# Lightning attention with a PReLU feed-forward: the written-out order of the first three chunks, written anew

## The chip, the cores and the metric

The kernel runs on one core of a Trainium2 chip. The core has five engines, each with a queue of its own that it works through in order: TensorE (PE, the matmuls; its weight loads are shown as PEld), VectorE (DVE), ScalarE (ACT), GpSimd (POOL) and SyncE (SP, which here only issues DMAs). The metric is the device time of one execution in microseconds (us). Results lie in SBUF, matmuls write into PSUM, and inputs and the output lie in HBM.

## What is computed

The inputs are q, k and v of shape (batch 4, heads 8, positions 768, width 64), one decay factor `lam` per head, and the feed-forward's `w_in` (512 x 2048), `w_out` (2048 x 512) and `alpha` (2048). Attention is linear with a decay, in blocks of 64 positions that hand a state on:

```python
intra = einsum('bhic,bhjc->bhij', qb, kb) * Dmask      # lam ** (i - j) for i >= j, else 0
intra = einsum('bhij,bhjd->bhid', intra, vb)
inter = einsum('bhid,bhde->bhie', qb * lam_pow, kv_state)
out[:, :, sl] = intra + inter
kv_state = lam_block * kv_state + einsum('bhsd,bhse->bhde', kb * rev_pow, vb)
```

The outputs of all heads side by side are the 3072 rows of x (512 wide), and the kernel's output is `g @ w_out` with `h = x @ w_in` and `g = max(h, 0) + alpha * min(h, 0)`, in float32.

## The kernel before

**Tiling.** The positions are taken in blocks of 128 here, two at a time. A chunk `c` (six of them) is 256 positions of two batches, thus 512 rows of x; a *unit* is one chunk, one batch and one half of the heads (four heads), so each chunk has four units, numbered 4c to 4c + 3. Of unit `n`, `units[n]` is the chunk, the batch within it and the half of heads. Units 0 and 1 are the first batch of chunk 0, units 2 and 3 the second; units 4 to 7 are chunk 1, 8 to 11 chunk 2.

**What a unit needs, and which function issues it:**
- `load` (L80): q, k or v of one batch in float32 into `kraw`, `qraw`, `vraw`; all eight heads, or four of them (`half` 0 or 1), by SP's queue or, with "G", by POOL's. `load_v16` (L272): v of one unit, turned into float16 on the way, always by POOL. `load_win`, `load_wout`: a quarter of `w_in` or `w_out`, by POOL.
- `cast` (L261): float32 to float16 of q or k (tile `qk`), on ACT ("A"), DVE ("V") or POOL ("G"), by way of `copy_on` (L246; ACT's instruction is L248, DVE's L250, POOL's L252).
- `transposed` (L328): four transposes of one of q and k on PE (L337) into a PSUM bank and a copy back to SBUF (tile `qkT`). `transposes` (L302) does both at once, on PE or, with "D", by a transposing DMA from SP.
- `key_decayed` (L285): k times its decay (tile `kdec`, L289), on POOL or DVE. `decayed` (L346): q times its decay (tile `qdT`, L351), on POOL, on DVE, or with "P" on DVE straight from the transposes' PSUM bank.
- `score_products` (L380): 16 small matmuls into the PSUM tile `s`, of which there is one (L387); `masked` (L395): `s` times the decay mask, on DVE (L398, tile `sm`). `scores` is both.
- the state of a unit: 8 small matmuls for each of its two blocks (`state_products`, L432); in the first position pair, `states` (L451) then copies the first block's state on ACT (L471) and updates the second block's on DVE (L461, two instructions). `state` does both blocks, into a bank each; `state1` (L516) does one block into one bank. Both first zero the other half of the bank with two matmuls (`beside`, L498).
- the output of a unit: two matmuls with the state (`inter`, L371) and 16 with the masked scores (`intra`, L412), into the PSUM tile `acc`, of which there is one, and a copy of it to `xT` (`attended`, L441) on ACT or DVE.
- `cluster(old, new, eng)` (L474): the output of unit `old` (copied by `eng`), and scores and state of unit `new`, interleaved.

**The feed-forward.** `up(c, f)` (L527) makes 128 of the 2048 hidden columns of a chunk: four matmuls 512 wide (L532), ACT's negative part (L540) and DVE's combination with the slopes (L549). With `bi` it does one batch, half as wide. `down(c, t, part, 4)` (L556) adds a quarter of the hidden columns to one 128-row piece of the output (L562); the last quarter is followed by ACT's copy (L575) and a store by SP. `oma`, one minus the slopes, comes from `slopes` (L235: one small transpose on PE, one DVE instruction L238).

**Constants at the start.** From `lam`, ACT makes the decay vectors with exponentials: `query_decay` (L230), `key_decay`, `state_decay`, `decay_mask`; DVE makes the masks' logarithms (`mask_logs`, L198, two instructions L200 per call, four calls).

**Unread products.** `tick(n, bank)` (L146) and `fill(n, bank)` (L134) are matmuls whose result nobody reads: 128 columns wide (L150) and 512 wide (L138). They occupy PE and nothing else. 16 narrow ones on zeros stand ahead of everything.

**What sets the order.** The kernel is written under a manual schedule: each engine gets its instructions in the order in which the Python calls are made, and only semaphores wait between engines. Lines 633 to 934 are such a list, written out by hand: it interleaves the attention of chunks 0 to 4 (up to unit 18's casts) with the feed-forward of chunks 0 to 2, and says which engine takes each cast, copy or load and which PSUM bank each product goes to. The banks are `h` (two buffers), `op` and `tk` (one each); `s` and `acc` take the rest. From line 936 on a loop does chunks 3 to 5. `gate(i, "out")` (L115) is a tiny load on SP that waits for a part of `w_out`, so that what follows it on SP's queue stays behind.

Of the kernel before, what the change touches and what calls it, by code (L numbers as in the profile page):

```python
# [11 lines left out]
def kernel(  # L12
# [211 lines left out]
    def state_decay():  # L224
        nc.scalar.activation(rdecay, llp, AF.Exp, scale=float(L))
# [298 lines left out]
    G = {}  # L524
# [186 lines left out]
    load_v16(4)  # L711
    up(0, 5, None, "h")
    up(0, 4, 1, "tk")
    up(0, 2, None, "op")
    load(1, 1, "k", 1, "G")
    cast(4, "q16", "V")
    up(0, 3, None, "h")
    up(0, 0, None, "h")
    up(0, 6, None, "op")
# [12 lines left out]
    cast(7, "q16", "G")  # L732
    gate(2, "out")
    load_v16(7)
    transposed(4, 1, "V", "tk")
    cast(5, "q16", "G")
    load(2, 0, "k", 0)
    cast(5, "k16", "A")
    up(0, 11, None, "h")
# [237 lines left out]
```

## Time and profile before

| | |
|---|---|
| three runs | 211.89, 212.13, 212.15 us; median 212.13 |
| profiled execution | 211.88 us, of which 210.1 are the span from the first to the last instruction |
| PE busy | 204.2 us (97%) |
| DVE busy | 134.7 us (64%) |
| ACT busy | 111.5 us (53%) |
| POOL busy | 81.3 us (39%) |
| HBM | 27.27 MB read, 6.29 MB written |

In the profile, L12 is line 12 of the kernel; a helper's line stands for all its calls. A group of instructions has its engine, its operation, its tiles (written tile first), its shape and its count. `[0.35 <-ACT qk L248]` behind a row of the timeline says that the engine stood idle for 0.35 us ahead of it until ACT's instruction at L248 released it. PE's ends are modelled, so successive matmuls overlap in the rows; the distance from start to start is what one takes. The granted clock is PE's clock as a share of its full speed.

### The profile page before, as it was taken

The page shows a single profiled execution, that of the slowest core. Times are in us where ns is not written, and L with a number is a line of the kernel's source. Part 1 is how long each engine was busy: PE and PEld are TensorE (multiplying, and loading weights), DVE is VectorE, ACT ScalarE, POOL GpSimd, SP SyncE. Part 2 cuts the span into 40 slices and gives each one's busy share as a digit, 9 for nine tenths or more (in the row PEclk, how much of TensorE's full clock was granted, in tenths as well). Part 3 has the DMA queues.
Part 4 walks back from the last instruction along what each step waited for, and adds up shares of the span by engine and source line. Part 5 has one row for each costly group of instructions (what it writes and reads, how often), then busy time and mean ns, then how long its engine had stood idle before and what let it go on. Part 6 is the DMA issues. An engine that isn't in the chain of part 4 may idle for free.

```text
span 210.1 us, 5186 instructions
## 1 busy us (share of the span) xinstructions
PE 204.2 (97%) x2131; PEld 109.0 (52%) x2131; DVE 134.7 (64%) x230; ACT 111.5 (53%) x203; POOL 81.3 (39%) x111
## 2 busy tenths in 40 slices
PE   7989999999999999999999999999999999999993
PEld 7666445556444565555555455454554444444453
DVE  7998987456898959899964664664745444444000
ACT  7966697047677046677654554554444443443121
POOL 8999599233743422752880664421000000000000
PEclk9999999999999999999999999999999999999999
DMA  6999999999999979999496794224101101110212
GB/s 166 274 198 252 269 229 200 242 239 263 287 148 290 135 189 194 276 195 260 94 236 156 208 235 104 62 41 100 53 0 53 50 0 50 50 55 0 100 50 100
DMA packets 56315, 32.06 MB, mean 153 GB/s; under 512 B 23508, under 2 KB 52580, under 8 KB 56292
## 3 DMA queue, kind: packets, MB, share of 16 engines
q1 hardware_dynamic: 44788, 22.82, 44.8%
q0 software_dynamic: 11488, 8.91, 24.7%
q8 instruction: 16, 0.26, 0.5%
q14 instruction: 7, 0.06, 0.1%
q10 hardware_dynamic: 16, 0.00, 0.0%
HBM read 27.27 MB, written 6.29 MB: 160 GB/s over the span
## 4 chain that ended last, share of the span: by engine, by line
PE 93%; DVE 3%; ACT 1%; issue 0%; ACTq 0%
PE h_ps L532 40%; PE o_ps L562 34%; PE o_ps L585 7%; PE s L387 4%; PE acc L412 3%; PE acc L371 2%; PE tpx L337 1%; DVE dmask L200 1%; PE acc L432 1%; PE unread L138 1%; ACT L178 1%; DVE sm L398 1%; DVE kdec L289 1%; ACT xT L248 1%; DVE qk L250 0%
## 5 line engine op out<-in xcount | busy, mean ns | idle before, releaser
L549 DVE SCALAR_TENSOR_TENSOR g<-m,oma,h_ps 128x512 f16<-128x512 f32 (+1 forms) x97 | 70.9, 741 | 47.1 <-ACT m L540 44.6
L532 PE MATMUL h_ps<-xT,w_in_sb 128*128 128x512 f16 (+1 forms) x388 | 92.3, 377 | 0.0
L540 ACT ACTIVATE m<-h_ps 128x512 f32<-128x512 f32 (+1 forms) x97 | 57.4, 593 | 51.3 <-PE h_ps L532 51.0
L562 PE MATMUL o_ps<-w_out_sb,g 128*128 128x512 f16 x320 | 79.5, 379 | 0.0
L532 PEld LDWEIGHTS <-w_in_sb 128*128 128x128 f16 x388 | 37.3, 98 | 42.9
L562 PEld LDWEIGHTS <-g 128*128 128x128 f16 x320 | 30.0, 98 | 33.8
L398 DVE TENSOR_TENSOR sm<-s,dmask 128x1024 f16<-128x1024 f32 x24 | 29.3, 1220 | 9.5 <-PE s L387 9.3
L351 POOL TENSOR_TENSOR qdT<-qkT,qdecay 128x512 f16<-128x512 f16 (+1 forms) x19 | 18.9, 999 | 24.1 <-PE h_ps L532 14.6
L289 POOL TENSOR_TENSOR kdec<-kraw,kdecay 128x512 f16<-128x512 f32 x18 | 19.1, 1061 | 13.5 <-DMA kraw<-in_k_dram 13.5
L575 ACT ACTIVATE o_sb<-o_ps 128x512 f32<-128x512 f32 (+2 forms) x26 | 14.7, 565 | 18.1 <-PE o_ps L585 10.9
L248 ACT ACTIVATE xT<-acc 128x512 f16<-128x512 f32 x21 | 12.5, 596 | 18.0 <-PE acc L432 15.5
L461 DVE SCALAR_TENSOR_TENSOR R<-R,rdecay,acc 128x128 f16<-128x128 f16 x56 | 16.1, 339 | 0.5 <-ACT R L471 0.5
L252 POOL CAST v<-vraw 128x512 f16<-128x512 f32 x11 | 6.9, 628 | 21.3 <-DMA vraw<-in_v_dram 21.3
L585 PE MATMUL o_ps<-w_out_sb,g 128*128 128x512 f16 (+2 forms) x96 | 14.1, 308 | 0.0
L585 PEld LDWEIGHTS <-g 128*128 128x128 f16 x96 | 8.1, 98 | 6.1
L387 PE MATMUL s<-qkT 64*64 64x128 f16 x384 | 10.1, 222 | 0.2 <-DVE qkT L250 0.2
L412 PE MATMUL acc<-sm,v 64*64 64x128 f16 x384 | 9.8, 217 | 0.4 <-issue 0.4
L276 POOL DMA_DIRECT2D v<-in_v_dram x12 | 9.3, 780 | 0.2 <-issue 0.2
L371 PEld LDWEIGHTS <-R 128*128 128x128 f16 x80 | 6.2, 98 | 5.5 <-ACT xT L248 0.6
L371 PE MATMUL acc<-qdT,R 128*128 128x128 f16 x80 | 8.4, 220 | 0.4 <-ACT xT L248 0.4
L252 POOL CAST qk<-kraw 128x512 f16<-128x512 f32 x13 | 8.0, 612 | 1.7 <-DVE g L549 1.2
L387 PEld LDWEIGHTS <-qkT 64*64 64x64 f16 x384 | 6.3, 106 | 2.9 <-ACT qk L248 0.4
(69 smaller groups left out, 126.6 us busy)
## 6 DMA issues: line engine op xcount, KB each, us to landing
out_dram<-o_sb SPq DMA_DIRECT2D x23, 256.0 KB, 2.1
kraw<-in_k_dram SPq DMA_DIRECT2D x12, 256.0 KB, 5.0
qraw<-in_q_dram SPq DMA_DIRECT2D x10, 256.0 KB, 5.0
qraw<-in_q_dram SPq DMA_DIRECT2D x4, 512.0 KB, 5.5
w_in_sb<-in_moe_w_in_dram POOLq DMA_DIRECT2D x4, 512.0 KB, 8.5
w_out_sb<-in_moe_w_out_dram POOLq DMA_DIRECT2D x4, 512.0 KB, 10.3
vraw<-in_v_dram SPq DMA_DIRECT2D x4, 512.0 KB, 6.2
kraw<-in_k_dram SPq DMA_DIRECT2D x3, 512.0 KB, 5.1
```

Of the source, the lines that this page charges most:

```text
L289: engine(eng).tensor_tensor(out=kdec, in0=kr, in1=kdecay[:, ds(4 * hh, 4), :].rearrange("p h e -> p e h").unsqueeze(3).to_broadcast([128, ...
L351: engine(eng).tensor_tensor(out=qdT[:, :, :, p], in0=(t["qps"] if eng == "P" else t["qkT"][:, 0])[:, :, :, p], in1=qdecay[:, hh, :, :, p], ...
L371: nc.tensor.matmul(ot[a][:, hp, :].rearrange("p (e j) -> p e j", e=2), lhsT=R[bb, ho, 2 * pbo + a][:, hp].rearrange("p l d -> p (l d)"), r ...
L387: nc.tensor.matmul(t["s"][ds(a * 64, 64), hl, hp, 1 - e, :].rearrange("p (e j) -> p e j", e=2), lhsT=t["qkT"][p, 1, e, hp, ds(a * 64, 64)] ...
L398: nc.vector.tensor_tensor(out=t["sm"].rearrange("p a h x j -> p (a h) x j"), in0=t["s"].rearrange("p a h x j -> p (a h) x j"), in1=mask_of ...
L412: nc.tensor.matmul(ot[a][ds(hl * 64, 64), hp, :], lhsT=t["v16"][p, 2 * hp + hl, e, :], rhs=t["sm"][p, hl, hp, 1 - e, :], start=(2 * pb + a ...
L461: nc.vector.scalar_tensor_tensor(out=R[b, hh, m + 1][:, hp], in0=R[b, hh, m][:, hp], scalar=rdecay[:, 2 * hh + hp : 2 * hh + hp + 1], in1= ...
L532: nc.tensor.matmul(h_ps[:, 0:n] if bi is None else h_ps[:, 0:n].rearrange("p (e j) -> p e j", e=2), lhsT=w_in_sb[:, gi, ts(f, 128)], rhs=x ...
L540: nc.scalar.activation(m[:, 0:n], h_ps[:, 0:n], AF.Relu, scale=-1.0)
L549: nc.vector.scalar_tensor_tensor(out=g, in0=mv, scalar=oma[:, f : f + 1], in1=hv, op0=ALU.mult, op1=ALU.add)
L562: nc.tensor.matmul(o_ps, lhsT=lhs(c, f, t), rhs=w_out_sb[:, f, :], start=(f == 0), stop=(f == NF - 1),)
L585: nc.tensor.matmul(o_ps[:, 0:n], lhsT=lhs(c, f, t), rhs=w_out_sb[:, f, ds(x, n)], start=(f == 0), stop=(f == NF - 1),)
```

## The change

Lines 633 to 934, the list, are replaced by a list of the same calls in another order and partly on other engines, banks and queues; no function is changed. The calls that make up the work of chunks 0 to 2 are the same but for these points:

- the narrow unread products, 24 and 22 in two places, are 6 and 56 ahead of the first transpose; the wide ones, seven, are three
- unit 3's state is two `state1` calls in place of one `state`; unit 6's scores and state are calls of their own in place of a part of a cluster
- the first output (unit 1) is copied by ACT in place of DVE, unit 0 keeps ACT
- q of chunk 0's second batch is loaded in two halves in place of whole; of chunk 1 and later, some loads are whole that were halves and the other way round, and one key half of unit 6 goes by SP's queue in place of POOL's
- v of unit 11 is loaded as float32 and cast on POOL in place of being turned on the way
- casts, decayed keys, decayed queries and copies change engines in many places; `slopes` stands ahead of the first scores; `up` of one tile of chunk 1 is done in two halves

The diff from its start to the first `up`, and the later places that the prediction speaks of:

```diff
--- before
+++ after
                 a[i]()
                 i += 1
 
+    load(0, 1, "k", 0, "G")
+    query_decay(3, 1)
     query_decay(2, 1)
-    load(0, 1, "q", None, "G")
+    mask_logs(2)
+    tick(6, "tk")
+    load(0, 1, "q", 0, "G")
+    mask_logs(0)
+    key_decay()
+    state_decay()
+    load(0, 0, "k", None)
+    cast(0, "k16", "V")
     query_decay(0, 1)
-    load(0, 0, "k", None)
-    tick(24, "h")
+    load(0, 0, "q", None)
+    key_decayed(0, "V")
     mask_logs(1)
-    load(0, 0, "q", None)
-    load(0, 1, "k", 0, "G")
-    key_decay()
+    key_decayed(1, "V")
+    decay_mask(2)
+    decay_mask(0)
+    cast(1, "k16", "V")
+    tick(56, "tk")
+    load(0, 1, "q", 1, "G")
     load_v16(1)
+    decay_mask(1)
+    cast(1, "q16", "A")
+    mask_logs(3)
+    query_decay(1, 1)
+    cast(0, "q16", "V")
+    transposed(1, 1, "V", "h")
+    decay_mask(3)
+    query_decay(0, 0)
+    load_alpha()
     load(0, 1, "k", 1, "G")
-    mask_logs(2)
-    state_decay()
-    query_decay(1, 1)
-    cast(1, "k16", "A")
-    mask_logs(0)
-    mask_logs(3)
-    decay_mask(1)
     load_v16(0)
+    transposed(1, 0, "V", "h")
     load_v16(2)
-    key_decayed(0, "V")
-    cast(1, "q16", "A")
-    cast(0, "k16", "V")
-    transposed(1, 1, "V", "tk")
+    transposed(0, 1, "V", "op")
+    transposed(0, 0, "A", "tk")
     load_v16(3)
     load_win(1)
-    tick(22, "h")
-    key_decayed(1, "G")
-    decay_mask(0)
-    cast(0, "q16", "V")
-    decay_mask(2)
-    decay_mask(3)
-    query_decay(3, 1)
-    transposed(1, 0, "V", "h")
-    cast(3, "q16", "A")
-    transposed(0, 1, "A", "h")
-    transposed(0, 0, "V", "op")
-    scores(1)
-    fill(7, "tk")
+    slopes()
     load_win(0)
     decayed(1, "P")
+    cast(2, "q16", "A")
+    scores(1)
+    fill(3, "op")
     key_decayed(2, "G")
-    cast(2, "q16", "A")
     cast(2, "k16", "A")
+    cast(3, "q16", "G")
+    transposed(2, 0, "V", "op")
+    state1(1, "h", 0)
+    decayed(2, "G")
+    cast(3, "k16", "A")
+    decayed(0, "G")
     scores(0)
-    cast(3, "k16", "G")
-    state1(1, "op", 0)
-    transposed(2, 1, "A", "tk")
-    transposed(2, 0, "V", "h")
-    cluster(1, None, "V")
-    decayed(0, "G")
+    transposed(2, 1, "A", "h")
+    key_decayed(3, "G")
+    cluster(1, None, "A")
+    load_win(3)
+    transposed(3, 0, "A", "h")
     state1(0, "op", 0)
+    load(1, 0, "q", 0, "G")
     scores(2)
-    transposed(3, 0, "A", "tk")
-    transposed(3, 1, "A", "h")
-    state1(2, "op", 0)
-    decayed(2, "G")
-    load_alpha()
-    key_decayed(3, "V")
-    load(1, 0, "q", 0, "G")
-    load_win(3)
-    state1(1, "h", 1)
+    transposed(3, 1, "A", "tk")
+    state1(2, "h", 0)
     decayed(3, "G")
+    load(1, 0, "k", 0, "G")
+    load(1, 0, "q", 1, "G")
+    load_win(2)
     cluster(0, None, "A")
+    load_v16(4)
+    load(1, 0, "k", 1, "G")
+    state1(1, "op", 1)
+    load_wout(0)
     scores(3)
-    state(3, "to")
-    load(1, 0, "k", None, "G")
-    load_win(2)
+    state1(3, "tk", 0)
     cluster(2, None, "A")
+    load(1, 1, "q", 1, "G")
+    state1(2, "op", 1)
+    state1(3, "tk", 1)
     state1(0, "h", 1)
-    load(1, 1, "q", 1, "G")
-    load(1, 0, "q", 1, "G")
-    load_wout(0)
-    state1(2, "tk", 1)
-    slopes()
+    cast(4, "q16", "G")
     cluster(3, None, "A")
-    up(0, 4, 0, "op")
+    load(1, 1, "k", 1, "G")
+    cast(5, "q16", "G")
+    up(0, 4, 0, "h")
+    cast(4, "k16", "G")
+    load_v16(5)
+    load_wout(1)
+    up(0, 6, None, "op")
...
+    load_wout(3)
+    up(0, 12, None, "op")
+    gate(2, "out")
+    transposed(4, 0, "A", "tk")
+    up(0, 13, None, "h")
+    load(1, 1, "k", 0)
+    up(0, 14, None, "h")
     key_decayed(4, "G")
-    up(0, 13, None, "tk")
-    up(0, 1, None, "h")
-    load_wout(1)
-    up(0, 15, None, "op")
-    load_v16(5)
-    cast(4, "k16", "A")
-    up(0, 12, None, "h")
-    load_wout(2)
-    transposed(4, 0, "A", "tk")
-    up(0, 14, None, "h")
-    up(0, 10, None, "op")
-    cast(7, "q16", "G")
-    gate(2, "out")
+    up(0, 15, None, "tk")
+    cast(5, "k16", "G")
     load_v16(7)
...
+    load(2, 0, "q", None)
+    up(0, 11, None, "op")
+    up(0, 8, None, "tk")
+    transposed(5, 0, "A", "h")
+    load(4, 0, "v", 0)
     up(0, 9, None, "h")
+    cast(7, "q16", "A")
+    load(2, 1, "q", 0)
+    cluster(None, 4, "A")
+    load(1, 1, "q", 0, "G")
+    down(0, 3, 0, 4, "h")
+    transposed(5, 1, "A", "tk")
+    transposed(7, 0, "A", "op")
+    cast(7, "k16", "A")
+    down(0, 0, 0, 4, "h")
+    down(0, 2, 0, 4, "tk")
     decayed(4, "G")
-    transposed(5, 1, "A", "op")
-    key_decayed(5, "G")
-    load(2, 0, "q", 0)
-    up(0, 8, None, "tk")
-    load_wout(3)
-    transposed(5, 0, "A", "h")
-    query_decay(2, 0)
-    cluster(None, 4, "A")
-    down(0, 3, 0, 4, "h")
-    load(1, 1, "q", 0, "G")
-    load(2, 1, "q", 1)
-    cast(7, "k16", "G")
-    transposed(7, 0, "A", "op")
-    down(0, 2, 0, 4, "tk")
-    transposed(7, 1, "A", "op")
-    load(1, 1, "k", 0, "G")
-    down(0, 0, 0, 4, "h")
+    query_decay(1, 0)
...
+    key_decayed(7, "V")
+    load_v16(6)
+    decayed(7, "V")
+    transposed(7, 1, "V", "op")
+    cluster(4, 5, "A")
     down(0, 1, 0, 4, "op")
-    load_v16(8)
-    key_decayed(7, "G")
-    cluster(4, 5, "V")
+    down(0, 3, 1, 4, "h")
     down(0, 2, 1, 4, "tk")
     down(0, 1, 1, 4, "op")
-    decayed(7, "G")
-    down(0, 3, 1, 4, "h")
     down(0, 2, 2, 4, "tk")
-    decayed(5, "G")
+    cast(6, "q16", "G")
+    decayed(5, "V")
+    down(0, 1, 2, 4, "op")
+    cluster(5, 7, "A")
+    load_v16(8)
+    cast(6, "k16", "V")
+    key_decayed(6, "V")
+    cast(8, "k16", "V")
+    key_decayed(8, "G")
...
+    cluster(7, None, "A")
+    scores(6)
+    state(6, "to")
+    down(0, 3, 3, 4, "h")
+    transposes(8, "V", False)
     down(0, 0, 2, 4, "h")
+    cast(11, "v16", "G")
+    gate(1, "out")
+    load(3, 0, "q", None)
+    load(2, 1, "k", None)
...
+    transposes(9, "D", False)
...
```

More of the change, by code (lines that the diff above doesn't have):

```diff
@@ L779 @@
+    load(2, 1, "v", 1)
     load(2, 0, "k", 1)
[L780 to L796 removed]
     cast(9, "k16", "G")
@@ new lines @@
+    up(1, 3, 0, "h")
+    load_v16(9)
+    cast(10, "q16", "G")
+    load(3, 1, "q", 0)
+    up(1, 15, None, "op")
+    cast(9, "q16", "A")
+    up(1, 6, None, "h")
+    transposes(9, "D", False)
+    decayed(8, "G")
+    query_decay(2, 0)
+    load(3, 1, "k", 0)
+    load(3, 1, "k", 1)
+    cast(10, "k16", "G")
+    load(3, 0, "k", None)
+    key_decayed(11, "G")
+    up(1, 0, None, "tk")
+    up(1, 11, None, "h")
+    up(1, 1, None, "op")
+    cast(11, "k16", "G")
+    query_decay(3, 0)
+    up(1, 2, None, "h")
@@ L857 @@
[L857 to L875 removed]
+    up(1, 3, 1, "tk")
@@ new lines @@
+    key_decayed(15, "G")
+    cluster(8, 9, "A")
+    cast(12, "k16", "V")
+    key_decayed(13, "V")
+    cast(13, "q16", "G")
+    load(2, 1, "q", 1)
+    decayed(9, "G")
+    cast(11, "q16", "G")
+    load(3, 0, "v", None)
+    down(1, 1, 0, 4, "h")
+    load(3, 1, "v", 1)
+    transposes(11, "D", False)
+    down(1, 0, 0, 4, "tk")
+    cast(14, "q16", "A")
+    key_decayed(14, "G")
+    up(1, 13, None, "op")
+    cast(12, "q16", "G")
+    decayed(10, "G")
+    down(1, 1, 1, 4, "h")
+    down(1, 0, 1, 4, "tk")
@@ new lines @@
+    load(4, 0, "q", 0)
+    cast(13, "k16", "G")
+    down(1, 2, 0, 4, "h")
+    down(1, 2, 1, 4, "h")
+    down(1, 1, 2, 4, "h")
+    decayed(11, "G")
+    cluster(9, 10, "A")
+    cast(16, "q16", "G")
+    down(1, 3, 0, 4, "op")
+    down(1, 0, 2, 4, "tk")
+    transposes(12, "D", False)
+    key_decayed(12, "G")
+    decayed(12, "G")
+    load(4, 0, "k", None)
+    load(3, 1, "q", 1)
+    down(1, 3, 1, 4, "op")
+    cluster(10, 11, "A")
+    load(3, 1, "v", 0)
+    cast(13, "v16", "A")
+    down(1, 2, 2, 4, "h")
@@ L906 @@
-    up(2, 1, None, "h")
-    down(1, 3, 3, 4, "op")
-    cast(17, "q16", "A")
-    load(4, 1, "q", 0)
-    cluster(13, 14, "A")
-    load(4, 1, "k", 1)
-    key_decayed(16, "G")
-    up(2, 15, None, "tk")
-    up(2, 0, None, "op")
+    cast(17, "q16", "G")
+    load(4, 1, "v", 1)
+    cluster(11, 12, "A")
+    down(1, 0, 3, 4, "tk")
+    transposes(15, "D", False)
+    up(2, 4, None, "h")
+    up(2, 14, None, "tk")
+    decayed(13, "V")
+    up(2, 5, None, "h")
+    cast(16, "v16", "A")
+    key_decayed(17, "G")
@@ new lines @@
+    up(2, 2, None, "h")
+    up(2, 0, None, "tk")
+    load(4, 1, "q", None)
+    cast(17, "k16", "G")
+    decayed(14, "G")
+    cast(16, "k16", "G")
+    load(4, 0, "v", 1)
+    cluster(12, 13, "A")
+    transposes(16, "D", False)
+    down(1, 3, 2, 4, "op")
+    up(2, 1, None, "h")
+    load(4, 1, "v", 0)
+    up(2, 15, None, "h")
+    load(4, 1, "k", None)
+    up(2, 8, None, "tk")
+    decayed(15, "G")
+    key_decayed(16, "G")
+    key_decayed(18, "G")
+    cluster(13, 14, "A")
+    down(1, 3, 3, 4, "op")
```

196 lines of the change are left out of this document (45 added, 151 removed).

## The prediction

> **What bounds the kernel now.** I read the span on the profile's page, then the waits of TensorE, then a table by stage. The columns of the table are the stage, its length, and busy time with instruction count of PE, PEld, DVE, ACT and POOL.
>
> ```profile
> span 210.1 us, 5186 instructions
> ```
> ```profile
> PE unread L150 <- DVE zeros L122: 1.1, 1, 1.1
> PE acc L412 <- issue: 0.4, 1, 0.4
> PE acc L371 <- ACT xT L248: 0.4, 2, 0.2
> PE tpx L337 <- ACT qk L248: 0.4, 1, 0.4
> PE s L387 <- DVE qkT L250: 0.2, 1, 0.2
> ```
> ```profile
> 18.27:33.00 14.73, 14.73 (x92) 7.54 (x84) 12.42 (x22) 11.33 (x22) 12.34 (x17) 1.00 1.23 244
> 33.00:52.40 19.40, 19.40 (x323) 11.12 (x321) 11.66 (x20) 9.34 (x18) 8.56 (x13) 1.00 1.18 239
> 52.40:105.00 52.60, 52.60 (x616) 27.19 (x614) 47.59 (x84) 32.03 (x58) 24.90 (x32) 1.00 1.03 207
> ```
>
> All five waits of PE lie ahead of 18.27 us, where the first `up` begins (rows below). From there PE is busy in every microsecond up to 105, at granted clock 1.00, and past that the code is the same. The list can therefore win in one place only: by bringing the first `up` forward. It can lose there, or by opening a wait behind it. I call the start of the first `up` U; now U = 18.27.
>
> What sets U? These are the rows of the timeline for DVE and PE (start, length, engine, line).
>
> ```profile
> 3.75 2.69 DVE L200 SCALAR_TENSOR_TENSOR dmask<-rel_f,loglam,drop 128x192 f32<-128x192 f32 x8
> 6.36 1.30 DVE L289 TENSOR_TENSOR kdec<-kraw,kdecay 128x512 f16<-128x512 f32 x1
> 7.59 0.41 DVE L250 CAST qk<-kraw 128x512 f16<-128x512 f32 x1
> 7.92 0.41 DVE L250 COPY qkT<-tpx 128x512 f16<-128x512 f16 x1
> ...
> 9.59 1.22 DVE L398 TENSOR_TENSOR sm<-s,dmask 128x1024 f16<-128x1024 f32 x1
> 10.73 0.41 DVE L351 TENSOR_TENSOR qdT<-tpx,qdecay 128x256 f16<-128x256 f16 x1
> 11.49 1.22 DVE L398 TENSOR_TENSOR sm<-s,dmask 128x1024 f16<-128x1024 f32 x1 [0.34 <-PE s L387]
> 12.63 0.41 DVE L250 COPY qkT<-tpx 128x512 f16<-128x512 f16 x1
> ...
> 13.56 1.22 DVE L398 TENSOR_TENSOR sm<-s,dmask 128x1024 f16<-128x1024 f32 x1
> 14.70 1.07 DVE L289 TENSOR_TENSOR kdec<-kraw,kdecay 128x512 f16<-128x512 f32 x1
> 15.70 0.59 DVE L461 SCALAR_TENSOR_TENSOR R<-R,rdecay,kv 128x128 f16<-128x128 f16 x2
> 16.22 1.21 DVE L398 TENSOR_TENSOR sm<-s,dmask 128x1024 f16<-128x1024 f32 x1
> ...
> 18.90 0.16 DVE L238 TENSOR_SCALAR oma<-at_ps 128x16 f32<-128x16 f32 x1
> ```
> ```profile
> 3.21 2.74 PE L150 MATMUL unread<-ident 128*128 128x128 f16 x24
> 6.30 0.60 PE L337 MATMUL tpx<-ident,qk 128*128 128x128 f16 x4 [0.35 <-ACT qk L248]
> 6.70 1.43 PE L150 MATMUL unread<-ident 128*128 128x128 f16 x22
> ...
> 11.02 0.42 PE L387 MATMUL s<-qkT 64*64 64x128 f16 x16
> 11.26 0.22 PE L498 MATMUL kv<-zeros 64*64 64x128 f16 x2
> 11.32 0.29 PE L432 MATMUL kv<-v,kdec 64*64 64x64 f16 x8
> ...
> 13.10 0.42 PE L387 MATMUL s<-qkT 64*64 64x128 f16 x16 [0.20 <-DVE qkT L250]
> ...
> 15.43 0.25 PE L412 MATMUL acc<-sm,v 64*64 64x128 f16 x3 [0.42 <-issue]
> ...
> 17.71 0.28 PE L371 MATMUL acc<-qdT,R 128*128 128x128 f16 x2 [0.18 <-ACT xT L248]
> ...
> 18.27 0.50 PE L532 MATMUL h_ps<-xT,w_in_sb 128*128 128x256 f16 x3
> ```
> ```profile
> 5.63 0.61 ACT L248 ACTIVATE qk<-kraw 128x512 f16<-128x512 f32 x1
> ...
> 17.06 0.60 ACT L248 ACTIVATE xT<-acc 128x512 f16<-128x512 f32 x1 [0.47 <-PE acc L412]
> ```
>
> DVE has work for all but fractions of 3.75 to 18.9. The four L398 rows, one masking per unit, are the spine: call their starts M1 = 9.59, M0 = 11.49, M2 = 13.56, M3 = 16.22 (units 1, 0, 2, 3). Between them stand other DVE jobs (an output copy, unit 3's decayed keys), so they are 1.90, 2.07 and 2.66 apart. U comes 2.05 after M3: the output of unit 2 on ACT ends at 17.06 + 0.60 = 17.66, unit 3's group starts at 17.71, and U is 0.56 later.
>
> **The change part by part, up to U.** Start to start, from the rows above, DVE pays 2.61 for eight mask logs (3.75 to 6.36), 1.23 for decayed keys, 0.33 for a cast or a copy.
>
> *Ahead of M1.* The new list puts on DVE, in this order: logs of two head pairs, cast k of unit 0, decayed keys 0, logs, decayed keys 1 (was POOL), cast k of unit 1 (was ACT), logs, cast q of unit 0, three copies of transposes, the slopes' `oma` (was at 18.90), unit 1's decayed queries (was behind M1). Sum: 3.75 + 2.61 + 2 x 1.23 + 3 x 0.33 + 3 x 0.33 + 0.16 + 0.41 = **M1 at 11.4**, 1.8 later than now. What they wait for is there: k of unit 0 is cast at 5.06, and now ACT casts from the same load at 5.63 with no wait shown.
>
> The price of decayed keys is the disputed one. POOL's row, and a DVE row at a time when POOL does nothing:
>
> ```profile
> 5.99 2.32 POOL L276 DMA_DIRECT2D v<-in_v_dram  x3
> ```
> ```profile
> 45.55 0.69 DVE L289 TENSOR_TENSOR kdec<-kraw,kdecay 128x512 f16<-128x512 f32 x1
> ```
>
> Beside POOL's DMA issues the job took 1.30, alone 0.69. The new list gives POOL ten issues in a row from 2.67, at 0.77 each up to 10.4, so both jobs (5.4 to 6.6, 7.3 to 8.5) lie beside issues. I take 1.23 for each; the other end is 0.6. The Trainium skill's page "SBUF — State Buffer", section "Who interferes with whom", says that a DVE instruction with two SBUF inputs is held up by a GpSimd instruction that reads SBUF, not by one that only writes, and infers that descriptor generation needs only the write side. By that both jobs would cost what the 45.55 row shows; the 6.36 row speaks against it, and rival B keeps it.
>
> *The unread products.* Now 24 + 22 narrow ones (0.114 and 0.065 us each) and seven wide; then 6 + 56 narrow and three wide. 62 x 128 + 3 x 512 against 46 x 128 + 7 x 512 columns is 9472 on both sides. From 3.21, half of the 62 at the slow pace and half at the fast one end near 8.7. The first transpose needs unit 1's cast, which DVE ends at 8.9, so they cost nothing; without that cover the price is 8.7 - 6.3 = 2.4 on the first transpose. The transposes end well ahead of DVE's copies at 9.8, 10.1 and 10.5.
>
> *M1 to M3.* With unit 1's output on ACT and unit 3's decayed keys on POOL, only one copy (0.33) stands between M1 and M0 and none between M0 and M2. The scores share one PSUM tile, so the loop is masking 1.22 + hand-over 0.06 (12.63 + 0.41 to 13.10) + scores to masking 0.47 (11.02 to 11.49) = 1.75. M0 = 13.15, M2 = 14.9. For M3 the loop gives 16.65, but unit 1's two R updates (0.52 together, 15.70 to 16.22) now stand ahead of it on DVE. They wait for a PE group behind unit 0's cluster, which waits for ACT's copy of unit 0's state. ACT's queue then holds, from 13.45: copy, output of unit 1, copy, state 0, copy, state 2, output of unit 0, about 0.5 per copy or output and 0.35 per state, so state 0 is done at 15.3, unit 0's cluster at 15.9, the updates run 16.4 to 16.9. **M3 = 16.9**; without the updates 16.65.
>
> *M3 to U.* Unit 0's output ends at 16.7, unit 2's cluster at 17.25, its output, behind unit 3's first state copy on ACT, at 18.05. Unit 3's group then starts at 18.1, and U = 18.1 + 0.56 = **18.65**. The masking ends at 18.1 and just fits. The two state groups of unit 3 in place of one are the same 20 matmuls; they and two others (0.28 each, 11.26 to 11.54) run while ACT holds unit 2's output. One addition: the row at 15.43 has a pause of 0.42 that nothing in the profile explains. Counted by matmuls (the 223rd), it would fall on unit 0's second group in the new list too, on the way to M3. Bounds: nothing, and 0.42 in full; I add 0.1, since what follows waits for ACT in part. So U = 18.75, bounds 17.4 (both decayed keys at 0.6: 2 x 0.62 less) and 19.05; half a microsecond later than now.
>
> **Behind U.** PE's work is the same but for unit 6, which gets scores and a state of its own with two more pairs of `beside` matmuls; a pair costs 0.06 (11.26 to 11.32), and splitting a cluster a little more: +0.15. Does a wait open?
>
> ```profile
> w_in_sb<-in_moe_w_in_dram POOLq DMA_DIRECT2D x4, 512.0 KB, 8.5
> ...
> kraw<-in_k_dram SPq DMA_DIRECT2D x12, 256.0 KB, 5.0
> ```
> ```profile
> 41.65 0.60 POOL L252 CAST qk<-qraw 128x512 f16<-128x512 f32 x1 [4.02 <-DMA qraw<-in_q_dram]
> ```
> ```profile
> 37.37 0.74 SPq L119 DMA_DIRECT2D gates<-w_out_sb  x1
> ```
>
> The loads up to the first weights move the same bytes (q in two halves), the first weights issued at 8.8 (behind one more issue) where now they follow the three at 8.3: 8.8 + 8.5 = 17.3, before U. The third block of w_in is then issued ahead of chunk 1's q and needed six `up` later, the fourth nine later; both gain slack. The long stretch of POOL waiting for unit 6's q (41.65) stays. On SP a key half of unit 6, formerly POOL's, now stands first behind the gate: 37.37 + 0.74 + 5.0 = 43.1, and its cast on DVE has its turn after unit 7's masking, near 45.7. Whole q of units 8 and 9 and an early half v of chunk 4 follow it; unit 8's cast is due near 50. DVE's added jobs of units 5 to 8 (eight, 0.33 to 0.69 each) fall into 33 to 52.4, where it is busy 11.66 of 19.40. I cost all of this at nothing; the cover is a microsecond or two, and unit 6's copy on ACT, behind an output copy of 0.6, has only some 0.2.
>
> **Sum.** 211.88 (the profiled execution: span 210.1 and 1.8 around it) + 0.48 + 0.15 = 212.5. The runs' median, 212.13, is 0.25 above that execution; I put on part of it: **212.6**. About 0.2%, 0.42 us, is what a measurement of this kernel can tell from no change.
>
> **Rivals.**
> - *B, faster:* the decayed keys on DVE cost 0.6 each. Then M1 = 10.15 and everything behind shifts with it, as ACT and PE wait for DVE or each other all along: U = 17.5, time 211.88 - 0.8 + 0.15 = 211.2. For it: the 45.55 row, and that page's rule. Against: the 6.36 row. It decides below about 0.8 per job.
> - *C, slower still:* a wait behind U. Unit 6's key half lands later than 46 instead of 43.1, its transposes, scores and state wait, then unit 8's. Price 0.6 to 1 on top: 213.3. For it: DMA is busy all through 33 to 52.4 (share 1.18), and five loads are queued on SP where now three are. Against: 2.5 us of room.
> - *D, no change:* the pause doesn't recur on the path and the R updates fit into the loop: U = 18.15, time 211.9 to 212.1.
>
> **Chances.** Forecast (212.1 to 212.9) 0.48; B 0.19; C 0.22; D 0.11. Faster by over 0.2%: B and a rest of D, 0.20. Within: D and the lower two fifths of the forecast, 0.29. Slower: 0.51. The range reaches from B to C, 211.1 to 213.4, and leaves out a larger gain, from an M1 nearer to 10, and two waits of C at once.
>
> **What would show it.** Right: L289 twice on DVE before 8.6 at over 1.0 each; the first L398 at 11.4 and the next two 1.75 apart; two L461 ahead of the fourth; the first L532 at 18.5 to 19.0; PE without waits behind it. Wrong: L289 at 0.7; the first transposes later than 9, if PE speeds up later than now and all 62 products go slowly (3.21 + 62 x 0.114 = 10.3); a PE wait near 47 to 51 on `qk` or `kdec`.

## The result and the profile after

The changed kernel takes 211.15 us (median of six runs, 210.67 to 211.33); the kernel before took 212.12 in six runs beside them (211.89 to 212.53). The ratio is 0.995, with a 95% interval of 0.994 to 0.996: **faster by half a per cent**, where 0.2% slower was forecast. The profiled execution is the fastest of the six, 210.67 us with a span of 208.8.

First the waits of TensorE after. Of the five before, three are gone, and none has come behind the first `up`.

```profile
PE unread L150 <- DVE zeros L122: 1.1, 1, 1.1
PE acc L371 <- ACT xT L248: 0.2, 1, 0.2
```

Next DVE's timeline up to the first `up`, and three rows of PE's.

```profile
5.07 0.42 DVE L250 CAST qk<-kraw 128x512 f16<-128x512 f32 x1
5.41 0.68 DVE L289 TENSOR_TENSOR kdec<-kraw,kdecay 128x512 f16<-128x512 f32 x1
6.01 0.74 DVE L200 SCALAR_TENSOR_TENSOR dmask<-rel_f,loglam,drop 128x192 f32<-128x192 f32 x2
6.66 0.68 DVE L289 TENSOR_TENSOR kdec<-kraw,kdecay 128x512 f16<-128x512 f32 x1
...
9.99 1.21 DVE L398 TENSOR_TENSOR sm<-s,dmask 128x1024 f16<-128x1024 f32 x1
11.12 0.41 DVE L250 COPY qkT<-tpx 128x512 f16<-128x512 f16 x1
11.72 1.23 DVE L398 TENSOR_TENSOR sm<-s,dmask 128x1024 f16<-128x1024 f32 x1 [0.18 <-PE s L387]
13.46 1.23 DVE L398 TENSOR_TENSOR sm<-s,dmask 128x1024 f16<-128x1024 f32 x1 [0.52 <-PE s L387]
14.95 0.61 DVE L461 SCALAR_TENSOR_TENSOR R<-R,rdecay,kv 128x128 f16<-128x128 f16 x2 [0.26 <-PE kv L432]
15.47 1.22 DVE L398 TENSOR_TENSOR sm<-s,dmask 128x1024 f16<-128x1024 f32 x1
```
```profile
3.22 4.50 PE L150 MATMUL unread<-ident 128*128 128x128 f16 x62
7.74 1.38 PE L337 MATMUL tpx<-ident,qk 128*128 128x128 f16 x16
...
17.25 1.04 PE L532 MATMUL h_ps<-xT,w_in_sb 128*128 128x256 f16 x6
```

The four maskings start at M1 = 9.99, M0 = 11.72, M2 = 13.46, M3 = 15.47, and the first `up` at U = 17.25. Against before, M1 is 0.40 later, then each step is shorter: 1.73 for 1.90, 1.74 for 2.07, 2.01 for 2.66, 1.78 for 2.05. The sum, 0.40 - 0.17 - 0.33 - 0.65 - 0.27 = -1.02, is the difference between the two U, told along the maskings.

It doesn't say yet what held U. In both traces PE's last wait ahead of U is for ACT (`acc L371 <- ACT xT`), not for the fourth masking: units 0, 2 and 3 share one accumulator, and each output waits until ACT has copied the one before it. These are pieces of the chain that ended last in the kernel before (start, length, what), and then ACT's rows of after for the same two copies.

```profile
15.01 0.42 issue
15.72 0.61 ACT xT L248
16.66 0.38 PE acc L412 x16
17.06 0.60 ACT xT L248
```
```profile
14.71 0.60 ACT L248 ACTIVATE xT<-acc 128x512 f16<-128x512 f32 x1
16.03 0.60 ACT L248 ACTIVATE xT<-acc 128x512 f16<-128x512 f32 x1 [0.27 <-PE acc L412]
```

Unit 0's output starts on PE (its L371) at 14.38 before and at 14.02 after, 0.36 earlier. Its copy on ACT starts 1.34 behind that before and 0.69 after: in the kernel before PE's pause of 0.42 lies inside this output, in this execution of after there is none. From that copy to U are 2.55 and 2.54. So of the 1.02, 0.36 come from an earlier start of the outputs and 0.65 from the pause staying away. Without the pause, before's U would be held by the fourth masking instead, which ends at 16.22 + 1.21 = 17.43; with the 0.35 of the products behind it U would be 17.78. By this estimate about half of the gain is the new order and half the pause.

Behind U the two kernels take the same. The last copy of an output on ACT, after and then before, starts 205.94 - 17.25 = 188.69 and 206.95 - 18.27 = 188.68 behind U:

```profile
205.94 0.28 ACT L575 ACTIVATE o_sb<-o_ps 128x128 f32<-128x128 f32 x1 [0.61 <-PE o_ps L585]
```
```profile
206.95 0.28 ACT L575 ACTIVATE o_sb<-o_ps 128x128 f32<-128x128 f32 x1 [0.62 <-PE o_ps L585]
```

The table by stage of after (columns as in the prediction) has PE busy in every microsecond from U to 105 again. From U to the end are 208.8 - 17.25 = 191.55, before 210.1 - 18.27 = 191.83; what is left of that difference, 0.28, lies behind the last copy. It isn't in the last store either, whose packets end 1.49 behind that copy in both (at 207.43 and 208.44).

```profile
17.25:33.00 15.75, 15.75 (x122) 7.99 (x117) 13.17 (x22) 12.07 (x23) 14.41 (x20) 1.00 1.24 246
33.00:52.40 19.40, 19.40 (x299) 11.10 (x298) 14.10 (x27) 8.92 (x19) 4.79 (x7) 1.00 1.15 251
52.40:105.00 52.60, 52.60 (x620) 27.49 (x619) 43.70 (x77) 31.69 (x57) 33.17 (x40) 1.00 0.98 208
```

### The profile page after: what moved, and what is told of

Same layout as the page of the kernel before. It is cut to its first block, busy times and chain, and to the rows that moved or that the text cites. A ratio compares the mean times of both kernels' runs of the same rounds, so it can differ in the third digit from the quotient of the medians.

```text
span 208.8 us, 5229 instructions
## 1 busy us (share of the span) xinstructions
PE 204.3 (98%) x2151; PEld 109.8 (53%) x2151; DVE 132.0 (63%) x229; ACT 111.3 (53%) x204; POOL 84.3 (40%) x114
## 4 chain that ended last, share of the span: by engine, by line
PE 94%; DVE 3%; ACT 1%; ACTq 0%; issue 0%
PE h_ps L532 40%; PE o_ps L562 34%; PE o_ps L585 7%; PE s L387 4%; PE acc L412 3%; PE acc L371 2%; PE tpx L337 2%; DVE dmask L200 1%; PE acc L432 1%; ACT L178 1%; DVE kdec L289 1%; DVE qk L250 0%; PE unread L138 0%; PE kv L432 0%; PE kv L498 0%; DVE qkT L250 0%
## 5 line engine op out<-in xcount | busy, mean ns | idle before, releaser
L532 PEld LDWEIGHTS <-w_in_sb 128*128 128x128 f16 x392 | 37.8, 98 | 43.2
L351 POOL TENSOR_TENSOR qdT<-qkT,qdecay 128x512 f16<-128x512 f16 (+1 forms) x19 | 20.6, 1087 | 17.9 <-DMA qkT<-qk 8.0
L248 ACT ACTIVATE xT<-acc 128x512 f16<-128x512 f32 x24 | 14.3, 597 | 23.3 <-PE acc L432 21.0
L461 DVE SCALAR_TENSOR_TENSOR R<-R,rdecay,acc 128x128 f16<-128x128 f16 x54 | 15.5, 340 | 0.1
L252 POOL CAST qk<-qraw 128x512 f16<-128x512 f32 x12 | 7.6, 636 | 18.1 <-DMA qraw<-in_q_dram 18.1
L252 POOL CAST qk<-kraw 128x512 f16<-128x512 f32 x14 | 8.6, 614 | 8.4 <-DMA kraw<-in_k_dram 8.4
L252 POOL CAST v<-vraw 128x512 f16<-128x512 f32 x10 | 6.1, 615 | 10.4 <-DMA vraw<-in_v_dram 10.4
L371 PEld LDWEIGHTS <-R 128*128 128x128 f16 x80 | 6.2, 98 | 4.7 <-ACT xT L248 0.3
L276 POOL DMA_DIRECT2D v<-in_v_dram x11 | 8.6, 793 | 0.0
L371 PE MATMUL acc<-qdT,R 128*128 128x128 f16 x80 | 8.4, 219 | 0.2 <-ACT xT L248 0.2
```

Source lines behind the costliest of these rows:

```text
L252: nc.gpsimd.tensor_copy(out=out, in_=in_)
L351: engine(eng).tensor_tensor(out=qdT[:, :, :, p], in0=(t["qps"] if eng == "P" else t["qkT"][:, 0])[:, :, :, p], in1=qdecay[:, hh, :, :, p], ...
L371: nc.tensor.matmul(ot[a][:, hp, :].rearrange("p (e j) -> p e j", e=2), lhsT=R[bb, ho, 2 * pbo + a][:, hp].rearrange("p l d -> p (l d)"), r ...
L532: nc.tensor.matmul(h_ps[:, 0:n] if bi is None else h_ps[:, 0:n].rearrange("p (e j) -> p e j", e=2), lhsT=w_in_sb[:, gi, ts(f, 128)], rhs=x ...
```

## The experiments

Two theories stood at first: that the gain is all ahead of U, since the decayed keys on DVE cost 0.6 each and not 1.23; and, as a rival, that the new list behind U has a part in it.

**before_again.** No edit: the kernel before, profiled once more.

> The kernel before, unchanged, profiled once more. Two readings of its first profile are open: DVE's first decayed keys at 6.36 took 1.30 us where the kernel after paid 0.68, and PE paused 0.42 us at 15.01 for nothing that the profile shows. If both belong to the program, they are here again: a row of 1.30 on DVE near 6.4 and a pause of 0.3 to 0.5 near 15.0. If they are accidents of one execution, the decayed keys take 0.68 and the pause is gone or elsewhere; the time is 211.9 to 212.5 either way.

Measured: 212.01 in one run, U at 18.28, decayed keys at 6.36 in 1.31 again, and PE's pause of 0.4 on the way again. The slow row is no accident of one execution.

**new_front** and **old_front.** Each list up to the first `up`, with the other list's rest. A few calls are shifted at the seam, so that each call is made once:

```diff
-list of the kernel before, up to the first up
+new list, up to the first up               # new_front; old_front is the reverse
...
-    load_v16(4)                             # new_front: made in the new front,
...
-    load(1, 1, "k", 1, "G")                 # so left out of the old rest
...
-    cast(4, "q16", "V")
...
-    cast(5, "q16", "G")
...
-    query_decay(0, 0)
```

> The new list up to the first up, the old list from there on (without the five calls that the new front has done already). Theory: the whole gain lies ahead of the first up, so the time is that of the kernel after, 211.1 to 211.2, ratio 0.995 to 0.996, with the first up at 17.25. Rival: some of it comes from the rest of the list; then 211.4 to 211.9.

> The old list up to the first up, the new list from there on (with five calls of the new front put in at the seam or later). Theory: no gain, 212.0 to 212.3, ratio 0.999 to 1.001, first up at 18.3. Rival: the rest of the new list brings 0.2 to 0.6 of its own, 211.5 to 211.9.

Measured: new_front 213.07 (212.89 to 213.31), ratio 1.0044 [1.003, 1.0057]; old_front 213.16 (212.86 to 213.29), 1.0045 [1.0032, 1.0058]. Both miss, for one reason. The waits of PE show one behind U (it ends at 36.56 in new_front and at 29.56 in old_front); new_front's and old_front's row:

```profile
PE tpx L337 <- POOL qk L252: 1.2, 1, 1.2
```
```profile
PE tpx L337 <- POOL qk L252: 1.1, 1, 1.1
```

A cast of chunk 1 on POOL comes late in both: some microseconds earlier POOL's queue stands still, 3.28 in new_front and 5.99 in old_front, until a load of q lands, and the cast that PE needs is behind that. Apart from it the stages add up. In new_front U is 17.92, and from there 211.1 - 17.92 = 193.2 are left: before's 191.83, as it has the old rest, + 1.2 for the wait + 0.15. In old_front U is 18.60 (its first `up` writes bank `h`, and waits 0.25 for DVE's state updates that read it), and 211.4 - 18.60 = 192.8 are left: after's 191.55 + 1.1 + 0.15. So neither of these two hybrids shows the gain, and the new rest brings nothing of its own in them. What else new_front shows is why its U is later than after's, with the same calls ahead of it:

```profile
3.21 5.67 PE L150 MATMUL unread<-ident 128*128 128x128 f16 x62
8.72 0.50 PE L337 MATMUL tpx<-ident,qk 128*128 128x128 f16 x6
```

The same 62 unread products took 5.67 instead of 4.50. PE does them at about 0.107 us each at first and at 0.056 later, and it goes over at another moment in each execution: at 4.84 us in after's profile, at 7.28 here. So the first transposes start at 8.72 instead of 7.74, DVE idles 0.49 ahead of its copies, and M1 is 10.56.

**double_kdec.** The disputed job once more.

```diff
     key_decayed(1, "V")
+    key_decayed(1, "V")
```

> The kernel after, with the decayed keys of unit 1 made twice on DVE ahead of the first masking (the first result is not read). Theory: the start of the first up follows DVE's start of the first masking one to one, and decayed keys beside POOL's DMA issues cost 0.6 us there; the first masking moves from 9.99 to 10.6, the first up from 17.25 to 17.85, the time by 0.6 to 211.75. Rival 1, slack on ACT or PE takes part of it up: 0 to 0.3. Rival 2, the job is slowed beside DMA issues after all when it lies elsewhere among them: 1.2.

Measured: 211.82 (211.35 to 212.17, twelve runs), ratio 0.9981 [0.9971, 0.999], thus 0.67 more than after's median (the lowest runs, 211.35 and 210.67, lie 0.68 apart). DVE's rows of double_kdec:

```profile
6.66 1.28 DVE L289 TENSOR_TENSOR kdec<-kraw,kdecay 128x512 f16<-128x512 f32 x2
7.87 0.49 DVE L250 CAST qk<-kraw 128x512 f16<-128x512 f32 x1
...
10.66 1.21 DVE L398 TENSOR_TENSOR sm<-s,dmask 128x1024 f16<-128x1024 f32 x1
```

Two jobs in 1.21 from start to start, and M1 later by 0.67: **0.6 each**. What is added on DVE ahead of M1 goes into the time in full. In this profile U is 18.28, which is 1.03 later than after's: the rest, 0.37, is PE's pause, which lies on the way here (M2 to M3 is 2.38).

**few_ticks.** Are the 62 products still the cover that I took them for, or do they set the first transposes?

```diff
-    tick(56, "tk")
+    tick(36, "tk")
```

> The kernel after with 36 in place of 56 narrow unread products in the second call: 42 instead of 62 ahead of the first transpose. In three traces of the new front the products end at 7.5, 8.6 and 8.7, according to when PE goes over from 0.107 to 0.056 us each (4.9, 7.1, 7.3), and where they end late DVE stands idle ahead of its copies and the first masking starts at 10.6 instead of 10.0. Theory: that is what spreads the six runs over 210.67 to 211.33; 42 products end by 7.7 at the slow pace too, so the first masking is at 10.0 always, and the median falls to 210.7 to 210.9. Rival 1: with fewer products PE goes over later, and slow transposes and scores take back the gain: 211.0 to 211.5. Rival 2: the spread has another cause and nothing moves, 211.1 to 211.2.

Measured: **210.63** (210.55 to 210.71, five runs), ratio 0.993 [0.9918, 0.9942]. It beats both kernels, and the runs lie within 0.16 where after's lay within 0.66. PE's rows:

```profile
3.20 3.16 PE L150 MATMUL unread<-ident 128*128 128x128 f16 x42
7.76 1.38 PE L337 MATMUL tpx<-ident,qk 128*128 128x128 f16 x16 [1.40 <-DVE qk L250]
```

With 42 products PE is done 1.4 before DVE's cast when it speeds up early, as here; in the profile of out1_dve below, which has 42 as well, they run to 7.89, and the first transpose starts at 7.78 all the same. That the median of after lies 0.48 above its own profile fits executions in which the 62 end behind the cast, as in new_front. But no such execution of after itself was profiled, and 20 products fewer also move PE's pause from unit 0's output to the fourth scores (last section). What each has of the 0.48 is open.

**old_ticks.** The products placed as before the change, in the new list.

```diff
-    tick(56, "tk")
+    tick(18, "tk")
     transposed(1, 1, "V", "h")
+    tick(22, "tk")
-    fill(3, "op")
+    fill(7, "op")
```

> The kernel after with the unread products placed as before: 24 narrow ones ahead of the first transpose, 22 behind it, seven wide ones. One part undone. Theory: the first transpose, which waits for a cast that ends at 7.7, stays where it is, but the 22 stand ahead of the second one, 1.2 us at the fast pace and 2.4 at the slow one, and DVE's second copy waits for it: first masking 0.5 to 1.5 later, and four more wide products (0.86) where PE has no slack near 10.5: median 211.8 to 212.8. Rival: DVE is late anyway and PE has room; 211.1 to 211.4.

Measured: 213.82 (212.19 to 214.94, seven runs), ratio 1.0073 [1.0038, 1.0107]. PE's rows:

```profile
3.21 2.95 PE L150 MATMUL unread<-ident 128*128 128x128 f16 x24
7.72 0.61 PE L337 MATMUL tpx<-ident,qk 128*128 128x128 f16 x4 [1.56 <-DVE qk L250]
8.12 2.55 PE L150 MATMUL unread<-ident 128*128 128x128 f16 x22
10.46 1.49 PE L337 MATMUL tpx<-ident,qk 128*128 128x128 f16 x12
```

PE idles 1.56 after 24 products, does the 22 that follow at 0.11 each and goes over to the fast pace only at 13.59; M1 is 12.87. Three of the seven runs (213.79, 213.82, 214.66) have a mean granted clock of 0.992; the other four, at full clock, lie at 212.19 to 214.94. Even the lowest is 1.04 above after's median, where the whole change gains 0.97: the new list needs its products where they now stand.

**b_late_issues.** Does POOL's issuing slow DVE's job at 6.36? The kernel before, with no DMA issue on POOL between 6.0 and 9.6.

```diff
+    key_decayed(2, "G")
...
-    load_v16(0)
-    load_v16(2)
     key_decayed(0, "V")
...
+    tick(22, "h")
+    load_v16(0)
+    load_v16(2)
     load_v16(3)
     load_win(1)
-    tick(22, "h")
     key_decayed(1, "G")
...
-    key_decayed(2, "G")
```

> The kernel before, with POOL's three v loads and the first weights' load issued behind the decayed keys of units 2 and 1, so that POOL issues no DMA between 6.0 and 9.6. What made DVE's first decayed keys take 1.31 us at 6.36 (twice in two traces), when the kernel after paid 0.68 beside issues of the same kind? If POOL's issues do it, the row is 0.69 now. If ACT's exponentials and casts or the landing loads do it, it stays at 1.3. The time is of no interest here: loads come late.

In the edit the four loads stand behind unit 2's decayed keys, but still ahead of unit 1's.

Measured: 217.34 in one run, which only says that POOL's queue comes late: it stands 3.64 for unit 2's k, and PE waits 3.6 for decayed keys behind it. POOL issues nothing from 6.02 to 10.66. The row at stake:

```profile
6.36 0.68 DVE L289 TENSOR_TENSOR kdec<-kraw,kdecay 128x512 f16<-128x512 f32 x1
```

0.68 instead of 1.31 at the same moment, on the same data: **POOL's issues had caused it.** The transfers under way were about the same, 103 packets between 6.3 and 7.7 us where the kernel before has 108, so it wasn't they.

**b_swap.** Is it the job or the moment? The kernel before, with a cast ahead of the decayed keys.

```diff
-    key_decayed(0, "V")
     cast(1, "q16", "A")
     cast(0, "k16", "V")
+    key_decayed(0, "V")
```

> The kernel before, with the cast of unit 0's k ahead of unit 0's decayed keys on DVE, so that these start at 6.69 instead of 6.36. If what slowed them is a matter of the moment (an issue's phase, a landing load), the row changes by tenths from 1.31, down to 0.69 at best; if it is a matter of the job at this place of the order, it stays 1.3.

Measured: 212.4 in one run. DVE's rows:

```profile
6.36 1.42 DVE L250 CAST qk<-kraw 128x512 f16<-128x512 f32 x1
7.69 0.67 DVE L289 TENSOR_TENSOR kdec<-kraw,kdecay 128x512 f16<-128x512 f32 x1
```

Now the cast, 0.41 elsewhere, takes 1.42, and the decayed keys behind it 0.67 although POOL goes on issuing. **It isn't the job**: each of the two that started at 6.36, first behind the eight logs, was held for some 0.6 to 1.0. Whether the moment counts or the place behind the logs, these runs don't separate.

The last four runs start from few_ticks and each take back one part.

**out1_dve.** The first output is copied by DVE again.

```diff
-    cluster(1, None, "A")
+    cluster(1, None, "V")
```

> The kernel after with 42 narrow products (210.63) and the first output copied by DVE again, as before. One part undone on the quiet version. Theory: the copy, 0.68, comes on DVE between the second and the third masking, where DVE now waits 0.52 for the scores; the third masking is some 0.1 to 0.2 later, ACT is freed of 0.5 on its way to unit 0's state, and the outputs' chain (unit 0, 2, 3, with one accumulator) starts no later: 210.5 to 210.8. Rival: the maskings carry the time and the copy costs its 0.6 in full: 211.2.

Measured: 210.52 (210.51 to 210.70, five runs), ratio 0.9926 [0.9915, 0.9938], the same as few_ticks within their spreads. DVE's rows:

```profile
11.76 1.23 DVE L398 TENSOR_TENSOR sm<-s,dmask 128x1024 f16<-128x1024 f32 x1 [0.19 <-PE s L387]
12.90 0.68 DVE L250 CAST xT<-acc 128x512 f16<-128x512 f32 x1
13.51 1.22 DVE L398 TENSOR_TENSOR sm<-s,dmask 128x1024 f16<-128x1024 f32 x1
```

The copy just fits where DVE else idles 0.52 for the scores. This part of the change is worth nothing; before, a copy of transposes stood there too.

**state3_whole.** Unit 3's state in one call again.

```diff
-    state1(3, "tk", 0)
+    state(3, "to")
     cluster(2, None, "A")
...
-    state1(3, "tk", 1)
```

> The kernel after with 42 narrow products and unit 3's state in one call again, ahead of unit 2's output. One part undone. Theory: the same matmuls, but the ten of the second block now stand ahead of unit 2's group on PE and the two R updates of unit 3 ahead of unit 2's on DVE; unit 2's group comes 0.1 to 0.25 later and the chain of outputs with it: 210.7 to 210.9. Rival: nothing waits for it, 210.6.

Measured: 212.41 (211.62 to 216.01, twelve runs), ratio 1.0017 [0.999, 1.0045]; six runs at full clock lie at 211.62 to 211.72, the other six, at 213.11 to 216.01, have a mean granted clock of 0.984 to 0.992. In the profile (211.66) the maskings are where they were, but PE has a new wait and U is 18.31, 0.94 later than in few_ticks:

```profile
15.61 0.24 PE L498 MATMUL kv<-zeros 64*64 64x128 f16 x2 [0.40 <-DVE R L461]
...
17.26 0.24 PE L498 MATMUL kv<-zeros 64*64 64x128 f16 x2 [0.71 <-DVE R L461]
...
18.31 1.04 PE L532 MATMUL h_ps<-xT,w_in_sb 128*128 128x256 f16 x6
```

Unit 3's second block needs bank `op`, which DVE's updates of unit 1 still read (0.40), and unit 2's second block then needs the same bank, which the updates of unit 3 read, behind the fourth masking on DVE (0.71). With the blocks apart, unit 2's output goes ahead of these waits. So the state by blocks is worth 0.9 to 1.0 in this list.

**early_m1.** Unit 1's decayed keys on POOL and its cast on ACT, as before the change: 0.93 off DVE ahead of M1.

```diff
+    cast(1, "k16", "A")
...
-    key_decayed(1, "V")
...
-    cast(1, "k16", "V")
...
     load_win(1)
+    key_decayed(1, "G")
```

> The kernel after with 42 narrow products, unit 1's decayed keys on POOL again (behind the first weights' load) and the cast of unit 1's k on ACT again (behind the third decay vector). That takes 0.93 us off DVE ahead of the first masking. Theory A, my prediction's spine (the maskings on DVE carry U one to one): the first masking starts 0.6 to 0.9 earlier and the time falls to 209.7 to 210.1. Theory B: POOL's queue takes its place; its decayed keys of units 1 and 2 and the cast of unit 3's q come a microsecond later, PE waits for that cast ahead of unit 3's transposes, and the time is 210.9 to 211.5.

Measured: 211.38 (211.37 to 211.39, five runs), ratio 0.9965 [0.9952, 0.9978], 0.75 slower than few_ticks. M1 is 9.58 and M0 11.31, both 0.43 earlier. It isn't 0.6 or more, since DVE now waits 0.34 for the transposes, behind 42 products that run to 7.79 here. Then POOL is late, and PE waits for it twice:

```profile
13.04 0.40 PE L337 MATMUL tpx<-ident,qk 128*128 128x128 f16 x4 [0.89 <-POOL qk L252]
...
17.50 0.27 PE L371 MATMUL acc<-qdT,R 128*128 128x128 f16 x2 [0.48 <-POOL qdT L351]
```

M2 is 14.01 and U 18.05. POOL's queue is what a job taken off DVE would delay.

**late_r.** Unit 1's last state updates behind the fourth scores, so that M3 needn't wait for them.

```diff
-    state1(1, "op", 1)
     load_wout(0)
     scores(3)
+    state1(1, "op", 1)
```

> The kernel after with 42 narrow products and unit 1's second state block behind unit 3's scores, so that its two R updates no longer stand ahead of the fourth masking on DVE. My prediction had M3 delayed by them (16.9 instead of 16.65). Theory A, the maskings carry U: the fourth masking starts 0.26 earlier, and U and the time fall by 0.2 to 0.26, to 210.4. Theory B, the outputs of units 0, 2 and 3 through the one accumulator carry U (0.6 on ACT and 0.7 on PE each): the fourth masking is earlier, U and the time stay, 210.6.

Measured: 211.73 (211.54 to 213.31, twelve runs), ratio 0.9999 [0.9978, 1.002]; eight runs lie at 211.54 to 211.89, the other four, at 213.03 to 213.31, have a mean granted clock of 0.992. M3 is 15.19, 0.30 earlier than in few_ticks. But the updates now stand behind that masking (16.33 on DVE), and PE needs their bank:

```profile
16.98 0.24 PE L498 MATMUL kv<-zeros 64*64 64x128 f16 x2 [1.00 <-DVE R L461]
```

An earlier M3 came with a later U (18.75 in the profile, part of it at half clock; at full clock the time is some 0.9 above few_ticks): a wait that neither theory had.

## Why the prediction was wrong

**The step that failed is the price of the decayed keys beside POOL's issues.** I took 1.23 for each of two jobs ahead of M1; they took 0.60 each from start to start, in after and in double_kdec. That is 2 x 0.63 = 1.26 of the 1.5 by which U came earlier than forecast (17.25 for 18.75), and decides the sign. The premise held: POOL issued from 2.67 to 10.4, and both jobs lie beside issues, as after's rows show.

```profile
5.10 0.77 POOL L276 DMA_DIRECT2D v<-in_v_dram  x1
5.83 0.77 POOL L87 DMA_DIRECT2D kraw<-in_k_dram  x1
6.58 2.39 POOL L276 DMA_DIRECT2D v<-in_v_dram  x3
```

What failed is the inference from one row that such company always costs 0.6. The row was a special case, in which the issues held whatever DVE started just then (b_late_issues, b_swap). All the profiles together have 26 decayed keys on DVE with nothing but DMA issues beside them on POOL: 23 took 0.67 to 0.69, and three took 1.30 or 1.31, all at 6.36 in the old order. I had the other end, 0.6, from the 45.55 row, and chose the end that looked nearer in kind; one row in such company is not a price. Of the Trainium skill's page "SBUF — State Buffer", section "Who interferes with whom", this is left: its rule gave the right price here, yet b_late_issues speaks against its inference that descriptor generation leaves such DVE instructions alone, 0.68 without issues against 1.31 with them.

**The rest of M1** came 0.12 earlier than its sum: with 0.60 per job that gives 10.11, measured 9.99. I had put in `oma` and the decayed queries at their durations, 0.16 and 0.41; from start to start they took 0.08 and 0.33.

**M1 to U** was right: 1.73 and 1.74 for the loop of 1.75, 2.01 for the 2.0 of the updates ahead of M3, 1.78 for 1.75; and unit 2's copy on ACT ends 1.16 behind M3, for 1.15 in the forecast. The pause of 0.42, of which I added 0.1, did not fall on the path in this profile. In double_kdec it did, in unit 0's output as I had counted (M2 to M3 2.38). What I didn't see is that the pause also sets the 18.27 of the kernel before, for some 0.5 by the estimate above. That it stayed away in the profile of after is luck, for which the forecast had only bounds.

**The unread products** "cost nothing" was half right, and it leaned on the failed price: the cast that was to cover them ends at 7.26 + 0.42 = 7.68, not at 8.9. In the profile they end at 7.72, just then; in new_front the first transpose starts 0.98 later than in after. And I gave them no use: old_ticks is 1.0 to 3.8 slower than after's median, with its products placed as before and its clock full.

**Behind U** I added 0.15; up to the last copy it cost 0.01, and no wait opened. The 0.28 by which after is shorter behind that copy was in no term. The cover held in the list as a whole, though the two hybrids show how little shift in POOL's queue opens a wait of 1.1.

**Rival B** (0.6 per job) had the price right. That its 211.2 meets the median, 211.15, is in part luck: like my forecast it was worked out for the profiled execution, and that took 210.67, with U at 17.25 where B has 17.5 and with nothing of the 0.15 behind U. The median lies 0.48 higher for reasons that B didn't have. Rival C's wait did not come, and D's U of 18.15 was passed; by D's own conditions, 0.1 for the pause and 0.25 for the updates, it should have been 18.4. The measured time lies in the range.

**Which parts of the change do it.** Read along the maskings, unit 3's decayed keys and the copies left DVE's stretch between them (0.98 less from M0 to M3), for which M1 pays 0.40; read along the outputs, about half of the 1.02 at U is the pause, by the estimate above. Neither was tried by itself: no run puts unit 3's decayed keys back or takes the pause out of the kernel before. Single reversals show that the state by blocks (0.9 to 1.0) and the products ahead of the first transpose (1.0 and more) are needed in this list, and that the first output on ACT (0) is not. q in halves wasn't tried by itself either.

## What to carry to other kernels

A duration from a single row beside some company is a sample, not a price: look for the same instruction in other company, or take the company away in one run, before letting the worse row decide a sign. On a path shared by several engines, moving the first link forward is no gain until the queue behind the receiving engine and the bank that the next product writes have been followed too: early_m1 and late_r both brought a masking forward and ended later. Work that only keeps an engine busy has a right amount and place: here 42 products ahead of the first transpose did better than 62, and they end about when the real work arrives even in an execution in which they run slowly; 24 there with 22 behind it did worse than either. And before a gain is put down to an order, ask whether a wait that no one planned, like PE's pause, lies on the chain in one of the two traces only.

## What the runs showed of the hardware

**POOL's DMA issues hold DVE at certain moments.** The same decayed keys took 0.68 and 1.31, a cast 0.41 and 1.42, by whether POOL was issuing at 6.36 us (b_late_issues, before, b_swap). What an issue holds, and for which part of its 0.77 us, stays open: in after, jobs starting 0.31 and 0.08 behind an issue were not held, in before the one starting 0.37 behind was.

**PE's early pace.** Narrow products go at about 0.107 us and later at 0.056, while the granted clock of the profile says 1.00 in both stretches (after, 3.22 to 4.84 and 4.84 to 7.72). The change came at 4.35 to 7.6 us in all new lists but one, and at 13.59 in old_ticks, where PE had idled 1.56 after 24 products. The count of products isn't what sets the moment: with 62 of them it was 4.84 and 7.28. What does is open.

**The clock can fall back.** In late_r's profile the table by stage shows a granted clock of 0.50 from 17.31 to 20.72, right behind the wait of 1.00 quoted above:

```profile
17.31:20.72 3.41, 3.41 (x49) 2.05 (x42) 2.12 (x7) 0.98 (x2) 3.41 (x5) 0.50 1.22 246
20.72:40.00 19.28, 19.28 (x185) 10.09 (x184) 16.21 (x26) 14.26 (x27) 10.93 (x16) 1.00 1.26 234
```

b_late_issues has 0.50 from 13.4 to 20.2, around PE's wait of 3.6. Of the other variants, state3_whole and old_ticks have runs with a mean of 0.984 to 0.992, of which none was profiled. In all four PE has a wait ahead of the first `up` that after doesn't have: 1.00, 3.6, 0.40 with 0.71, and 1.56. But that such a wait causes it was not tried, and early_m1 with 0.89 and 0.48, and few_ticks with 1.40, have none of it.

**The pause without a releaser** is tied to a place in PE's row of matmuls. In double_kdec it is back, inside the 16 products of this row, which else take 0.42:

```profile
14.91 0.80 PE L412 MATMUL acc<-sm,v 64*64 64x128 f16 x16
```

Counted in the traces, it lies between the 223rd and the 224th matmul wherever it shows: in before, before_again, old_front, b_swap and double_kdec, where that is unit 0's output, and in few_ticks, where with 20 products fewer it is in the fourth scores (16 matmuls in 0.60 instead of 0.42). The DMA queue named "instruction" has a transfer of 16 KB that starts 2.28 to 2.46 us before the 224th matmul in these six: at 13.1 in before and double_kdec, at 12.65 in few_ticks. In the other eight, without the pause, the 224th starts 2.38 or more behind it; in after the transfer is at 11.8 and the matmul at 14.38. So PE may be waiting for instructions that are still being loaded. This is an argument from fourteen profiles; no experiment moved the transfer.
